# Moving a transposition from DRAM back to TensorE, and the send of wo's blocks two slots forward, in a fused attention and feed-forward kernel

## The chip, the cores and the metric

One core of one Trainium2 chip. The metric is device time in microseconds (us); lower is better. The kernel before takes 1171.03 us, the median of three runs (1169.38 to 1172.58).

## The reference, cut to what matters

x has 2048 rows of 576 numbers. Each row is normalised; the normalised rows feed both a windowed attention (32 heads of 18; each row attends to itself and to seven earlier rows at a distance of two) and a feed-forward layer of 4608 units. All is float32.

```python
xn = _layernorm(x, axis=-1)
return x + _A_ref(xn, A_wqkv, A_wo) + _B_ref(xn, B_w1, B_w2)
# _A_ref: qkv = xn @ wqkv; softmax over 8 keys (dilation 2); o @ wo
# _B_ref: relu(xn @ w1) @ w2
```

## The kernel before, in words

**Numbers.** Every float32 matrix is split into a high and a low part (`fp32r`): ScalarE writes the high part as a copy, VectorE subtracts it from the original for the low part. A product is high x high + high x low + low x high. So each value that TensorE reads needs ScalarE first and then VectorE.

**Stages.** The rows are dealt into two parities (`ph`, 0 and 1: even and odd rows of x), since the attention's distance of two never mixes them. One parity is 1024 rows: eight tiles `i` of 128 rows, or four blocks `tb` of 256. Work goes through *slots* `n` of the list `slots`: 2 parities x 12 chunks of the 4608 units x 4 blocks x 3 groups of 128 units, 288 slots. The second parity starts at slot 144. In each slot TensorE does half of a pair's *first-layer product* (`h_two`, 14 or 13 pairs of matmuls, h for two slots at once, into `ph` or `pm` banks) and one *second product* (`o_two`, into the four `po` banks). At every third slot VectorE adds the four `po` banks to x (`o_out`, the line `x<-po`); the next slot's second product needs these banks again. From slot 7 of a parity, every 24 slots, eight slots also hold a pass for queries, keys and values (`qkv_tile`), for a quarter of the heads.

**Half arrays.** From slot 7 on, matmuls come in pairs (`mm_rows`): one in the upper 64 rows of TensorE's array, one in the lower 64, into two banks at once.

**The order.** All of it is written out by hand and kept as it stands (`manual_schedule`); each engine runs its own instructions in that order, and SP issues nearly all transfers, in order too. `at(n, f)` puts f into slot n ahead of the second product, `late(n, f)` behind it. Weights are loaded into five staging buffers about four loads ahead and split at their step (`run_splits`). Attention is background work on VectorE: `run_bg(margin)` takes the next operations from the list `bg` as long as VectorE's counted time stays below TensorE's counted time plus a margin.

**wo.** At slots 122, 125, 128, 131 of a parity (144 more in the second) the attention's output is multiplied by wo inside the second product, two tiles i at each. For that the output is transposed on the way: `wo_a` (VectorE turns blocks of 32x32, `tr<-qo`), `blocks_out` (four transfers to DRAM, `turned<-tr`, L358), `wo_f` (one transfer back, the *fetch*, `xn<-turned`, L549), `wo_s` (ScalarE's high part, `k<-xn`, L558; VectorE's low parts, L559 and L560). `WO_STEPS` tells how many slots ahead of the product each of the four stands, for even and odd i.

**x of the second parity.** Around slot 144 the eight tiles of the second parity are loaded, normalised, transposed and split (`xT`). Tiles 0 to 3 go as wo's blocks do: `norm_turned` (ScalarE, two passes), `xt_a` (VectorE turns blocks), `blocks_out` (`words<-pr`), `xt_f` (three transfers back), `xt_s` (split). Tiles 4 to 7 go through TensorE: `norm` (VectorE), `make_xt` (four transposes of 128x128 and one of 128x64 on the whole array, L303 and L304, into `pm`, then the split, L308 to L318). The eight tiles of the first parity are all made with `make_xt`, in the first seven slots.

**Banks.** The pool `ps_m` holds two banks (`pm`), each a tile of its own that is taken anew for every use.

Of the kernel before, what the change touches and what calls it, by code (L numbers as in the profile page):

```python
# [44 lines left out]

# [14 lines left out]
def tile_body(ctx: ExitStack, tc: tile.TileContext, x, wqkv, wo, w1, w2, out):  # L60
# [34 lines left out]
    turned = pool("turned", 4, space=bass.MemoryType.DRAM)  # L95
    ps_o = pool("ps_o", 4, space=PSUM)
    ps_h = pool("ps_h", 2, space=PSUM)
    ps_m = pool("ps_m", 2, space=PSUM)

    f32 = lambda ap: ap.bitcast(F32)  # L100

    ident = consts.tile([P, P], F32, name="ident")
    make_identity(nc, ident)
# [27 lines left out]
        return ins  # L131

    def dve(n):
        t["dve"] += (n + 130) / 960.0


    tasks = deque()
# [143 lines left out]

    def norm(ph, i, act=False):
        nm, r = MR.pop((ph, i))
        xn = tmp.tile([P, 640], F32, name="xn", bufs=3)[:, 0:D]
        if act:
            nc.scalar.activation(xn, X[ph, i], AF.Identity, bias=nm)
            nc.scalar.activation(xn, xn, AF.Copy, scale=r)
        else:
            nc.vector.tensor_scalar(xn, X[ph, i], nm, r, op0=ALU.subtract, op1=ALU.mult)
            dve(600)  # L290
        XN[ph, i] = xn

    def transpose_split(src, hi, mix, lo, bank=None, parts=False):

        if bank is ps_o:
            pa = ps_o.tile([P, 512], F32, name="po").rearrange("p (k c) -> p k c", k=KT)
            pb = ps_o.tile([P, 512], F32, name="po")[0:DR, 0:P]
        else:
            pa = ps_m.tile([P, KT, P], F32, name="pm")
            pb = ps_h.tile([P, TBN], F32, name="ph") if bank is ps_h else ps_m.tile([P, P], F32, name="pm")  # L300
            pb = pb[0:DR, 0:P]
        for k in range(KT):
            nc.tensor.transpose(pa[:, k, :], src[:, k * P : (k + 1) * P], ident)  # L303
        nc.tensor.transpose(pb, src[:, KT * P : D], ident)  # L304
        t["pe"] += 5 * 0.06

        def high():
            nc.scalar.activation(hi, pa, AF.Copy)  # L308

        def low():  # L310
            nc.vector.tensor_tensor(lo, pa, f32(hi), op=ALU.subtract)
            dve(512)

        def last_high():
            nc.scalar.activation(mix[0:DR], pb, AF.Copy)

        def last_low():
            nc.vector.tensor_tensor(mix[DR:P], pb, f32(mix[0:DR]), op=ALU.subtract)  # L318
            dve(128)

        steps = high, low, last_high, last_low
        if not parts:
            for f in steps:
                f()
        return steps

    def make_xt(ph, i, bank=None, parts=False):
        tb, h = divmod(i, 2)
        if h == 0:
            XT[ph, tb] = xtp.tile([P, 10, TBN], F32R, name="xT")  # L330
        d = XT[ph, tb][:, :, h * P : (h + 1) * P]
        xn = XN.pop((ph, i))
        steps = transpose_split(xn, d[:, 5:9, :], d[:, 4, :], d[:, 0:4, :], bank, parts)
        if ph:
            nc.scalar.activation(d[DR:P, 9, :], f32(d[0:DR, 4, :]), AF.Copy)
        return steps

    def twin(tb):
        nc.scalar.activation(XT[0, tb][DR:P, 9, :], f32(XT[0, tb][0:DR, 4, :]), AF.Copy)
# [13 lines left out]
    def blocks_out(ph, i):  # L353

        td, tr = TD[ph, i]
        for r in range(4):
# [6 lines left out]
    def norm_turned(ph, i):  # L363
        nm, r = MR.pop((ph, i))
        z = prp.tile([P, W, UD], F32, name="pr").rearrange("p w c -> p (w c)")
        XN[ph, i] = xn, _ = z[:, 0:D], z[:, D : 2 * D]
        nc.scalar.activation(xn, X[ph, i], AF.Identity, bias=nm)
        nc.scalar.activation(xn, xn, AF.Copy, scale=r)

    def xt_a(ph, i):  # L370

        xn, tr = XN.pop((ph, i))
        nc.vector.transpose(tr, xn)
        dve(D)
        TD[ph, i] = turned.tile([D // 32, 32, P], F32, name="words"), tr

    def xt_f(ph, i):
        tb, h = divmod(i, 2)
        if h == 0:
            XT[ph, tb] = xtp.tile([P, 10, TBN], F32R, name="xT")  # L380
        z, td = f32(XT[ph, tb][:, 0:5, h * P : (h + 1) * P]), TD.pop((ph, i))[0]
        nc.sync.dma_start(z[:, 0:KT], td[0 : 4 * KT].rearrange("(k c) j i -> (c j) k i", k=KT))
        for rows in slice(0, DR), slice(DR, P):
            nc.sync.dma_start(z[rows, KT], td[4 * KT : D // 32].rearrange("c j i -> (c j) i"))

    def xt_s(ph, i):

        tb, h = divmod(i, 2)
        d = XT[ph, tb][:, :, h * P : (h + 1) * P]
        mix, z = d[:, 4, :], d[:, 9, :]  # L390
        nc.scalar.activation(d[:, 5:9, :], f32(d[:, 0:4, :]), AF.Copy)  # L391
        nc.vector.tensor_tensor(d[:, 0:4, :], f32(d[:, 0:4, :]), f32(d[:, 5:9, :]), op=ALU.subtract)
        nc.scalar.activation(z[DR:P], f32(mix[DR:P]), AF.Copy)
        nc.vector.tensor_tensor(mix[DR:P], f32(mix[DR:P]), f32(z[DR:P]), op=ALU.subtract)
        nc.scalar.activation(mix[0:DR], f32(mix[0:DR]), AF.Copy)
        dve(512)
        dve(128)

    TD = {}

# [5 lines left out]
    def qkv_tile(ph, u, i):  # L406
# [18 lines left out]

        if not second:
            for h in range(2):
                PQ[h] = ps_m.tile([P, 3, UD], F32, name="pm")
# [20 lines left out]
    def attention(ph, u):  # L449
# [129 lines left out]
    def h_terms(n, terms, other=False):  # L579
        ph, c, tb, f = slots[n]  # L580
        w, xt = W1[ph, c, f], XT[ph, tb]
        if n not in HP:
            HP[n] = ps_m.tile([P, TBN], F32, name="pm") if other else ps_h.tile([P, TBN], F32, name="ph")
# [31 lines left out]
    def h_two(g, second):  # L615


        def run(n, terms):
            ph, c, tb, f = slots[n]
            w, xt = W1[ph, c, f], XT[ph, tb]  # L620
            return [
                (HP[n], w[:, b // 5, (b % 5) * P : (b % 5 + 1) * P], xt[:, a, :], not second and j == 0, second and j == len(terms) - 1, TBN)
                for j, (a, b) in enumerate(terms)
            ]

        if not second:
            HB["m"] = not HB["m"] and not busy_m.intersection((g - 3, g - 2, g - 1))
            for n in (g, g + 1):
                HP[n] = ps_m.tile([P, TBN], F32, name="pm") if HB["m"] else ps_h.tile([P, TBN], F32, name="ph")
# [43 lines left out]
    def o_mm(n, out=True, which=range(2)):  # L673
# [18 lines left out]
        if out:  # L692
            o_out(n, which)

    def o_out(n, which=range(2), rows=False):
        ph, c, tb, f = slots[n]
        if f < C - 1:
# [8 lines left out]
        for k, h in order:  # L706
# [22 lines left out]
    for ph in range(NPH):  # L729
# [22 lines left out]
        if ph + 1 < NPH:  # L752
            e = b + SPP - SPC
            for i in range(NI):
                if i >= len(XT_STEPS):
                    z = e + 3 + 2 * i - (i == NI - 1)
                    at(z - 6, load_x, ph + 1, i)
                    at(z - 1, stats, ph + 1, i)
                    at(z, norm, ph + 1, i)
                    at(z + 1, make_xt, ph + 1, i)  # L760
                    busy_m.add(z + 1)
                    continue
                load, first, second, turn, send, back, parts = (e + k for k in XT_STEPS[i])
                at(load, load_x, ph + 1, i)
                late(first, stats, ph + 1, i, False, True)
                late(second, norm_turned, ph + 1, i)
                late(turn, xt_a, ph + 1, i)
                at(send, blocks_out, ph + 1, i)
                at(back, xt_f, ph + 1, i)
                at(parts, xt_s, ph + 1, i)  # L770
# [88 lines left out]
    def margin(n):  # L859
# [56 lines left out]
```

## Time and profile before

| what | value |
|---|---|
| median of the runs | 1171.03 us |
| the profiled execution | 1171.2 us |
| its span | 1169.5 us |
| TensorE (PE) busy | 1152.5 us, 99% |
| VectorE (DVE) busy | 804.8 us, 69% |
| ScalarE (ACT) busy | 287.7 us, 25% |
| the chain that ended last: TensorE's share | 93% |
| the same: transfers' share | 3% |
| granted TensorE clock, mean | 0.996 |

How to read it: the lines of the profile name a line of the kernel, the engine, the operation and `out<-in` by the tiles' names. PE is TensorE's matmul, PEld its loading of weights, SPq the queue in which SP issues transfers. TensorE's busy time includes matmuls that run at a lower clock, so a full row of it is not yet TensorE at its best; the pace of a slot in an undisturbed stretch is the measure. In a row of the windows view stand: the window, its length, busy time and count of PE, PEld, DVE, ACT and POOL, then the granted clock (1.00 is full), the transfers' share and GB/s. In a timeline row: start, length, engine, line, operation, count, and in brackets how long the engine had been idle and what ended it.

### The profile page before, as it was taken

To read this page: it belongs to the slowest core of one execution; us is meant where nothing else is said; L and a number is where in the kernel's file an instruction comes from. 1 tells how busy PE (TensorE), PEld (TensorE's weight loads), DVE (VectorE), ACT (ScalarE), POOL (GpSimd) and SP (SyncE) were. 2 spreads that over 40 slices of the span, in tenths; PEclk is the share of its full clock that TensorE was granted. 3 is DMA by queue.
4 is the path that set the end of the run, shared out by engine and by line. 5 is a ranking of instruction groups with operands and counts; after the bars stand their busy time and mean duration, and the time that the engine had idled before them with its cause. 6 is when DMAs were issued, how large, how long until landed. Compare 5 with 4: busy or idle time off the path is not lost.

```text
span 1169.5 us, 38344 instructions
## 1 busy us (share of the span) xinstructions
PE 1152.5 (99%) x17114; PEld 1142.7 (98%) x17114; DVE 804.8 (69%) x1457; ACT 287.7 (25%) x756; POOL 43.4 (4%) x60
## 2 busy tenths in 40 slices
PE   9999999999999999899999999999999999998998
PEld 8999999999999999899989999999999999998998
DVE  7428687878877888553663286977787878884533
ACT  5322222221222222121432122122222212221210
POOL 3200000000000000000010000000000000000000
PEclk9999999999999999999999999999999999999999
DMA  5312312311222212643552212122213222226502
GB/s 183 98 38 64 84 45 58 84 56 47 73 66 68 67 34 65 155 110 90 138 173 66 59 50 78 45 63 78 56 58 80 58 58 66 54 64 135 111 14 82
DMA packets 149940, 89.71 MB, mean 77 GB/s; under 512 B 58528, under 2 KB 133536, under 8 KB 149776
## 3 DMA queue, kind: packets, MB, share of 16 engines
q1 hardware_dynamic: 146816, 78.61, 25.5%
q10 hardware_dynamic: 2960, 8.65, 2.5%
q8 instruction: 135, 2.21, 0.8%
q14 instruction: 29, 0.24, 0.1%
HBM read 67.90 MB, written 11.14 MB: 68 GB/s over the span
## 4 chain that ended last, share of the span: by engine, by line
PE 93%; DMA 3%; SPq 1%; DVE 1%; ACT 1%; issue 1%; DVEq 0%; POOL 0%; ACTq 0%
PE po L129 40%; PE pm L129 27%; PE ph L129 22%; PE ph L119 1%; PE po L119 1%; DMA turned<-tr 1%; SPq L358 1%; DMA words<-pr 1%; DMA xn<-turned 1%; PE pm L303 1%; DVE x L709 0%; DMA xT<-words 0%; DMA x<-in_x 0%; DVE hlo L600 0%; SPq L179 0%
## 5 line engine op out<-in xcount | busy, mean ns | idle before, releaser
L129 PE MATMUL po<-w2t,hhi 64*128 64x256 f32 (+1 forms) x4448 | 450.5, 292 | 0.1
L129 PEld LDWEIGHTS po<-w2t,hhi 64*128 64x128 f32 x4448 | 365.0, 185 | 2.4 <-issue 1.2
L129 PE MATMUL po<-w2t,hlo 64*128 64x256 f32 (+1 forms) x2224 | 340.8, 290 | 0.0
L129 PE MATMUL ph<-xT,w1t 64*128 64x256 f32 x4698 | 303.4, 275 | 3.1 <-ACT xT L391 2.9
L129 PEld LDWEIGHTS ph<-xT,w1t 64*128 64x128 f32 x4698 | 291.0, 185 | 5.9 <-ACT xT L391 3.1
L709 DVE TENSOR_TENSOR x<-po,x 128x320 f32<-128x320 f32 (+1 forms) x384 | 149.7, 450 | 175.6 <-PE po L129 172.9
L129 PEld LDWEIGHTS po<-w2t,hlo 64*128 64x128 f32 x2224 | 224.3, 185 | 0.0
L129 PE MATMUL pm<-wq,xT 64*128 64x432 f32 x1728 | 180.6, 354 | 0.0
L129 PE MATMUL pm<-xT,w1t 64*128 64x256 f32 x2808 | 177.9, 273 | 0.0
L129 PEld LDWEIGHTS pm<-xT,w1t 64*128 64x128 f32 x2808 | 171.9, 184 | 0.0
L129 PEld LDWEIGHTS pm<-wq,xT 64*128 64x128 f32 x1728 | 162.5, 184 | 2.0
L597 ACT ACTIVATE hhi<-ph 128x256 fp32r<-128x256 f32 x183 | 60.8, 382 | 326.2 <-PE ph L129 294.2
L600 DVE SCALAR_TENSOR_TENSOR hlo<-ph,hhi 128x256 fp32r<-128x256 f32 x183 | 69.3, 417 | 75.6 <-ACT hhi L597 75.3
L597 ACT ACTIVATE hhi<-pm 128x256 fp32r<-128x256 f32 x105 | 34.7, 382 | 259.8 <-PE pm L129 259.3
L465 DVE TENSOR_TENSOR pr<-qo,k 128x1152 f32<-128x1152 f32 x64 | 84.9, 1350 | 2.0 <-DMA k<-k 2.0
L468 DVE TENSOR_REDUCE lg<-pr 128x64 f32<-128x1152 f32 x64 | 84.7, 1344 | 0.0
L497 DVE TENSOR_TENSOR pr<-lg,v 128x1152 f32<-128x1152 f32 x64 | 83.9, 1347 | 0.1
L434 ACT ACTIVATE k<-pm 128x144 f32<-128x144 f32 x64 | 19.3, 302 | 238.0 <-PE pm L129 191.1
L600 DVE SCALAR_TENSOR_TENSOR hlo<-pm,hhi 128x256 fp32r<-128x256 f32 x105 | 39.6, 418 | 44.3 <-ACT hhi L597 43.1
L504 DVE TENSOR_TENSOR pr<-pr 128x288 f32<-128x288 f32 (+1 forms) x128 | 69.7, 599 | 0.0
L166 DVE TENSOR_TENSOR w2t<-st,w2t 128x576 fp32r<-128x576 f32 x72 | 53.9, 749 | 16.2 <-ACT w2t L162 16.2
L166 DVE TENSOR_TENSOR w1t<-st,w1t 128x640 fp32r<-128x640 f32 x70 | 56.9, 812 | 2.2 <-ACT w1t L162 1.3
(87 smaller groups left out, 706.3 us busy)
## 6 DMA issues: line engine op xcount, KB each, us to landing
st<-in_w SPq DMA_DIRECT2D x72, 288.0 KB, 2.9
st<-in_w SPq DMA_DIRECT2D x72, 256.0 KB, 3.0
st<-in_wqkv SPq DMA_DIRECT2D x32, 216.0 KB, 3.1
turned<-tr SPq DMA_DIRECT2D x64, 80.0 KB, 2.9
xn<-turned SPq DMA_DIRECT2D x16, 320.0 KB, 3.3
st<-in_w SPq DMA_DIRECT2D x144, 32.0 KB, 2.7
out<-x SPq DMA_DIRECT2D x15, 288.0 KB, 2.5
x<-in_x SPq DMA_DIRECT2D x14, 288.0 KB, 4.1
```

Of the source, the lines that this page charges most:

```text
L119: nc.tensor.matmul(o, l, r, start=start, stop=stop)
L129: ins = nc.tensor.matmul(o, l[z], r[z], start=start, stop=stop)
L166: nc.vector.tensor_tensor(lo, src, f32(hi), op=ALU.subtract)
L303: nc.tensor.transpose(pa[:, k, :], src[:, k * P : (k + 1) * P], ident)
L434: nc.scalar.activation(k[:, W - 1 + j, :], pq[:, 1, :], AF.Copy)
L465: nc.vector.tensor_tensor(pr[i], q, window(k, i), op=ALU.mult)
L468: nc.vector.tensor_reduce(lg[:, i], pr.pop(i).rearrange(heads, d=Dh), axis=AX.X, op=ALU.add)
L497: nc.vector.tensor_tensor(pr[i].rearrange(heads, d=Dh), e, window(v, i).rearrange(heads, d=Dh), op=ALU.mult)
L504: nc.vector.tensor_tensor(o, z[:, 0:n], z[:, n : 2 * n], op=ALU.add)
L597: nc.scalar.activation(hi, pt, AF.Relu)
L600: nc.vector.scalar_tensor_tensor(lo, pt, 0.0, f32(hi), op0=ALU.max, op1=ALU.subtract)
L709: nc.vector.tensor_tensor(acc[:, cols], PO[k, h], acc[:, cols], op=ALU.add)
```

## The change

1. wo's blocks are turned and sent two slots sooner (`WO_STEPS`); fetch and split stay where they are.
2. All eight tiles of the second parity go through TensorE, in halves of 64 rows: `make_xt_rows` transposes the upper and the lower 64 rows of a tile side by side, five pairs of 64x128 blocks, into both `pm` banks. `norm` writes the last 64 columns twice, so that the fifth block has the full width. `XT_STEPS` holds the slots of load, statistics, normalisation and transposition. The way through DRAM (`norm_turned`, `xt_a`, `xt_f`, `xt_s`) goes.
3. The two `pm` banks become one tile, taken once (`two_banks`); `bank_m` hands out its halves in turn, and all former uses of the pool go through it.
4. Finished rows of x are stored one slot later (`store`).
5. The background's count: 70 instead of 130 cycles for each operation, 520 for the two reductions over the window, and another margin beside the passes for queries, keys and values.

By the built programs, SP issues 462 transfers instead of 490; TensorE has 80 transposes of 64 rows instead of 20 on the whole array; `pm` holds 101 tiles of h instead of 105.

```diff
 XT_STEPS = (
-    (-6, 0, 1, 2, 3, 4, 7),
-    (-5, 1, 2, 3, 4, 5, 8),
-    (-3, 2, 3, 4, 5, 6, 10),
-    (3, 4, 5, 6, 7, 8, 11),
+    (-6, 1, 2, 4), (-5, 2, 3, 5), (-3, 4, 5, 7), (4, 6, 7, 9),
+    (4, 8, 9, 11), (7, 10, 11, 13), (8, 12, 13, 15), (10, 13, 14, 16),
 )
-WO_STEPS = ((-5, -4, -3, -1), (-4, -3, -2, -1))
+WO_STEPS = ((-7, -6, -3, -1), (-6, -5, -2, -1))
...
-    ps_m = pool("ps_m", 2, space=PSUM)
+    ps_m = pool("ps_m", 1, space=PSUM)
+    two_banks = ps_m.tile([P, 2, 512], F32, name="pm")
+    bank_turn = [0]
+    def bank_m(n):
+        bank_turn[0] += 1
+        return two_banks[:, bank_turn[0] % 2, 0:n]
...
     def dve(n):
-        t["dve"] += (n + 130) / 960.0
+        t["dve"] += (n + 70) / 960.0
...
     def norm(ph, i, act=False):
...
+        if ph:
+            nc.vector.tensor_scalar(xw[:, D:640], X[ph, i][:, KT * P : D], nm, r, op0=ALU.subtract, op1=ALU.mult)
...
-            pa = ps_m.tile([P, KT, P], F32, name="pm")
-            pb = ps_h.tile([P, TBN], F32, name="ph") if bank is ps_h else ps_m.tile([P, P], F32, name="pm")
+            pa = bank_m(512).rearrange("p (k c) -> p k c", k=KT)
+            pb = ps_h.tile([P, TBN], F32, name="ph") if bank is ps_h else bank_m(P)
...
+    def make_xt_rows(ph, i):
+        tb, h = divmod(i, 2)
+        if h == 0:
+            XT[ph, tb] = xtp.tile([P, 10, TBN], F32R, name="xT")
+        d = XT[ph, tb][:, :, h * P : (h + 1) * P].rearrange("p k (t c) -> p k t c", t=2)
+        xn = XN.pop((ph, i))
+        pt = two_banks[:, :, 0 : 5 * 64].rearrange("p t (k c) -> p k t c", k=5)
+        for k in range(5):
+            for t_, z in enumerate((slice(0, 64), slice(64, P))):
+                nc.tensor.transpose(pt[:, k, t_], xn[z, k * P : (k + 1) * P], ident[z, z])
+        nc.scalar.activation(d[:, 5:9], pt[:, 0:KT], AF.Copy)
+        nc.vector.tensor_tensor(d[:, 0:4], pt[:, 0:KT], f32(d[:, 5:9]), op=ALU.subtract)
+        nc.scalar.activation(d[0:DR, 4], pt[0:DR, KT], AF.Copy)
+        nc.scalar.activation(d[DR:P, 9], pt[DR:P, KT], AF.Copy)
+        nc.vector.tensor_tensor(d[DR:P, 4], pt[DR:P, KT], f32(d[DR:P, 9]), op=ALU.subtract)
...
-            bg.append((0 if f is sm_exp else n + 130, f, ()))
+            bg.append((0 if f is sm_exp else n + 520 if f in (sm_max, sm_sum) else n + 70, f, ()))
...
-            elif c == NCH - 1 and (k, h) in (order[-1], order[-2 if rows else 1]):
-                nc.sync.dma_start(o_v[ph, i], acc)
+            elif end and h == 0:
+                store(ph, i)
+            elif c == NCH - 1 and h == 1 and not end:
+                at(n + 1, store, ph, i)
...
-            return (1.8 if odd else 2.7) + 2.4 * qkv - 0.8 * due
-        return (2.5 if odd else 3.5) + 2.4 * qkv - 0.8 * due
+            return (1.8 if odd else 2.7 + 2.4 * qkv) - 0.8 * due + 1.6 * (odd and qkv)
+        return (2.5 if odd else 3.5 + 2.4 * qkv) - 0.8 * due + 1.6 * (odd and qkv)
```

More of the change, by code (lines that the diff above doesn't have):

```diff
@@ L283, in norm @@
         nm, r = MR.pop((ph, i))
-        xn = tmp.tile([P, 640], F32, name="xn", bufs=3)[:, 0:D]
+        xw = tmp.tile([P, 640], F32, name="xn", bufs=3)
+        xn = xw[:, 0:D]
         if act:
@@ L332, in make_xt @@
         xn = XN.pop((ph, i))
[L333 to L336, printed above, removed]
+        return transpose_split(xn, d[:, 5:9, :], d[:, 4, :], d[:, 0:4, :], bank, parts)
+    def make_xt_rows(ph, i):
[8 more added lines that the diff above has]
+                nc.tensor.transpose(pt[:, k, t_], xn[z, k * P : (k + 1) * P], ident[z, z])
+        t["pe"] += 5 * 0.06
+        nc.scalar.activation(d[:, 5:9], pt[:, 0:KT], AF.Copy)
[3 more added lines that the diff above has]
+        nc.vector.tensor_tensor(d[DR:P, 4], pt[DR:P, KT], f32(d[DR:P, 9]), op=ALU.subtract)
+        dve(512)
+        dve(128)
     def twin(tb):
@@ L361, in blocks_out @@
             )
[L363 to L397, printed above, removed]
     TD = {}
@@ L427, in qkv_tile @@
             for h in range(2):
-                PQ[h] = ps_m.tile([P, 3, UD], F32, name="pm")
+                PQ[h] = bank_m(3 * UD).rearrange("p (s c) -> p s c", s=3)
             PQ[2] = mm_rows((run(0, LOWER_MORE), run(1, UPPER_MORE)))
@@ L582, in h_terms @@
         if n not in HP:
-            HP[n] = ps_m.tile([P, TBN], F32, name="pm") if other else ps_h.tile([P, TBN], F32, name="ph")
+            HP[n] = bank_m(TBN) if other else ps_h.tile([P, TBN], F32, name="ph")
             HN[n] = 0
@@ L628, in h_two @@
             for n in (g, g + 1):
-                HP[n] = ps_m.tile([P, TBN], F32, name="pm") if HB["m"] else ps_h.tile([P, TBN], F32, name="ph")
+                HP[n] = bank_m(TBN) if HB["m"] else ps_h.tile([P, TBN], F32, name="ph")
             HB["ins"] = mm_rows((run(g, LOWER_MORE), run(g + 1, UPPER_MORE)))
@@ L754, in tile_body @@
             for i in range(NI):
[L755 to L770, printed above, removed]
+                for k, f in zip(XT_STEPS[i], (load_x, stats, norm, make_xt_rows)):
+                    at(e + k, f, ph + 1, i)
+                busy_m.add(e + XT_STEPS[i][-1])
     for step, f, a in sorted(plan, key=lambda z: z[0]):
```

5 lines of the change are left out of this document (4 added, 1 removed).

## The prediction

> **What bounds the kernel now.** I read the page first (busy shares), then TensorE's waits, then the chain of work, then the timeline around the gaps. All TensorE times below are of one profiled execution: its span is 1169.5 us, its own time 1171.2 us (1.7 us lie around the span), and the median of the runs is 1171.03 us, so sums are made against 1171.2.
>
> From the page, from TensorE's waits, and from the chain:
>
> ```profile
> span 1169.5 us, 38344 instructions
> PE 1152.5 (99%) x17114; PEld 1142.7 (98%) x17114; DVE 804.8 (69%) x1457; ACT 287.7 (25%) x756; POOL 43.4 (4%) x60
> ```
> ```profile
> PE po L129 <- ACT k L558: 7.5, 2, 4.0
> PE ph L129 <- ACT xT L391: 2.9, 1, 2.9
> ```
> ```profile
> 447.42 1.60 PE ph L129 x28
> 459.89 1.59 PE ph L129 x28
> ```
>
> TensorE is busy 99% of the span: it is the bound, and only what it loses can be won. It waits at three places (two at wo, one between the parities). The two chain rows stand four slots apart, so an undisturbed slot is (459.89 - 447.42) / 4 = 3.12 us: this is the measure for what a disturbed stretch loses.
>
> **Part 1: turned blocks for wo sooner.** The chain's rows of the first wo slot of each parity, a later wo slot, and the timeline's starts of the two:
>
> ```profile
> 490.91 10.07 PE po L129 x123
> ...
> 525.31 8.68 PE po L129 x132
> ...
> 1071.43 9.98 PE po L129 x108
> ```
> ```profile
> 486.14 0.31 PEld L129 LDWEIGHTS po<-w2t,hhi 64*128 64x128 f32 x4
> ```
> ```profile
> 1067.16 0.31 PEld L129 LDWEIGHTS po<-w2t,hhi 64*128 64x128 f32 x4
> ```
>
> The first wo slot's second product runs from 486.14 to 490.91 + 10.07 = 500.98, 14.84 us; undisturbed it takes 8.68. Lost: 6.2 us. In the second parity: 1081.41 - 1067.16 = 14.25, lost 5.6 us; 11.8 together. That is more than the 7.5 us of waits, since the clock falls behind each gap:
>
> ```profile
> 492.00:494.00 2.00, 2.00 (x22) 2.00 (x22) 0.84 (x2) 0.00 (x0) 0.00 (x0) 0.50 0.29 79
> ```
>
> (seventh number: granted clock 0.50). What makes it late is SP's queue:
>
> ```profile
> 471.82 0.38 SPq L174 DMA_DIRECT2D st<-in_w  x1
> ...
> 472.81 0.59 SPq L179 DMA_DIRECT2D st<-in_w  x1
> ...
> 478.65 0.48 SPq L190 DMA_DIRECT2D st<-in_w  x1
> 480.34 0.38 SPq L549 DMA_DIRECT2D xn<-turned  x1
> 480.81 2.64 SPq L358 DMA_DIRECT2D turned<-tr  x4
> 483.49 1.49 SPq L174 DMA_DIRECT2D st<-in_w  x1
> ...
> 485.59 0.59 SPq L179 DMA_DIRECT2D st<-in_w  x1
> 487.00 0.38 SPq L549 DMA_DIRECT2D xn<-turned  x1
> ```
> ```profile
> 490.12 0.74 ACT L558 ACTIVATE k<-xn 128x640 fp32r<-128x640 f32 x1 [5.55 <-DMA xn<-turned]
> ```
>
> The first fetch holds the queue until the first send has landed; only then the second send goes (480.81), its blocks land just ahead of 487.00, the second fetch goes, and ScalarE gets its words at 490.12. In the changed order both first sends stand ahead of two w1 loads and a w2 load (seven issues), the very first ahead of two w2 loads more, and the first fetch only comes behind these: neither fetch waits for a landing. What is late next is SP itself. The w2 load ahead of the first fetch goes at about 478.65 (there it followed a send too), 0.5; the fetch 0.4; the third send, four DMAs, 2.3 to 2.6; the three issues of a w1 load 1.6 (471.82 to 473.40) to 2.7 (483.49 to 486.18). So the second fetch goes between 483.4 and 484.9 instead of at 487.0. With the 3.1 us from there to ScalarE's start (487.00 to 490.12) and ScalarE's 0.74, the high words are there at 487.2 to 488.7, and TensorE asks for them half a microsecond after 486.14. I take the early end, as the w1 loads around the sends are mostly of the short kind, and 0.4 us for VectorE's low words behind them: 1.0 us of wait per parity (bounds 0, and 2.8). **11.8 - 2.0 = 9.8 us won** (bounds 6 to 11.8). The two sends moved forward delay two w2 loads behind them by 2.3 us each; those are split two slots (6.2 us) after they are issued, so this costs nothing.
>
> **Part 2: x of the second parity.** Timeline and windows from slot 136's first-layer product to slot 151's:
>
> ```profile
> 562.74:620.44 57.70, 54.69 (x790) 51.77 (x788) 38.77 (x93) 23.38 (x54) 6.11 (x10) 0.97 0.59 158
> ```
>
> Fifteen slots take 57.7 us instead of 15 x 3.12 = 46.8: 10.9 us lost, by the wait of 2.9 us and the lower clock after it, four blocks of full-array transposes, and two places where VectorE's adds to x come late. The cost of a block now:
>
> ```profile
> 602.94 0.42 PEld L303 LDWEIGHTS pm<-ident,xn 128*128 128x128 f32 x4
> 602.95 0.66 PE L303 MATMUL pm<-ident,xn 128*128 128x128 f32 x4
> ...
> 603.44 0.27 PE L304 MATMUL pm<-ident,xn 128*64 128x128 f32 x1
> 603.64 0.30 PEld L129 LDWEIGHTS po<-w2t,hhi 64*128 64x128 f32 x4 [0.20 <-issue]
> ```
>
> From 602.94 to 603.64, 0.70 us, with two changes between the whole array and halves in it. New: eight blocks of five pairs of half-array transposes, no change of form. No row shows such a pair. Below: half of a 128-column transpose (0.66 less one's own 0.27, by three: 0.13), so 0.065 x 5 = 0.3 us; above: the ten one after the other at 0.13, 1.3 us. The nearest row is the pair of half-array matmuls, 1.59 / 14 = 0.11 at 256 columns; I take 0.1 a pair, 0.5 a block, **4.0 us for eight** (2.6 to 10.4). The Trainium skill (TensorEngine Tiling (Array Packing), Key Properties) says that changing the tiling mode drains TensorE; the idle 0.20 in the last row agrees.
>
> The DMA round trip through DRAM goes (28 issues), so the 2.9 us wait goes with its clock; each transposition stands six or more slots ahead of its first use. What is late next is VectorE: it now makes each block within one slot. The group rows (operations listed by form):
>
> ```profile
> L311 DVE TENSOR_TENSOR xT<-pm,xT 128x512 fp32r<-128x512 f32 x11 | 7.6, 687 | 5.5 <-ACT xT L308 5.5
> ...
> L308 ACT ACTIVATE xT<-pm 128x512 fp32r<-128x512 f32 x11 | 6.6, 598 | 13.2 <-PE pm L303 13.0
> ...
> L289 DVE TENSOR_SCALAR xn<-x,mv,rstd 128x576 f32<-128x576 f32 x10 | 5.8, 576 | 1.6 <-POOL rstd L274 1.4
> ...
> L318 DVE TENSOR_TENSOR xT<-pm,xT 64x128 fp32r<-64x128 f32 x8 | 2.3, 284 | 0.2
> L315 ACT ACTIVATE xT<-pm 64x128 fp32r<-64x128 f32 x8 | 2.1, 258 | 0.0
> ```
> ```profile
> 395.71 0.66 ACT L597 ACTIVATE hhi<-pm 128x256 fp32r<-128x256 f32 x2 [4.37 <-PE pm L129]
> ```
> ```profile
> 403.06 1.55 DVE L709 TENSOR_TENSOR x<-po,x 128x256 f32<-128x256 f32 x4
> ```
>
> Slots 137 and 143 have a block, a normalisation and the adds to x. From the end of the first-layer product: ScalarE's two relus 0.8 (0.66 and a hand-over), its 512-column copy 0.6, VectorE's subtraction 0.69, then (in the built order both of ScalarE's 64-row copies wait for that subtraction) 2 x 0.26, 0.28, normalisation 0.58 and its 64 extra columns 0.2 (an estimate from the 0.28): 3.7 us and hand-overs. Then the adds, 1.55: done at 5.4. TensorE goes on for 0.5 (block), 1.53 (second product, the rest of a slot) and 1.59 us (next first-layer product) and needs the last banks a quarter of a product later, at 4.0: a wait of about 1.4 us at slots 138 and 144 each, and by the same count 0.6 around 146 to 148: **3.4 us**. So 10.9 - 4.0 - 3.4 = **3.5 us won** (bounds: -2.9 with the dear transposes, 8.3 with the cheap ones and free adds).
>
> **Part 3: the two spare banks as one tile.** This is no move of work, but it adds waits. In the built program TensorE's transposes of x tile 2 wait no longer for their own xn but for VectorE's hlo<-pm, which reads the *other* bank: the order treats the tile as one. Its start in the timeline:
>
> ```profile
> 13.87 0.60 PE L303 MATMUL pm<-ident,xn 128*128 128x128 f32 x4
> ...
> 15.71 0.42 DVE L600 SCALAR_TENSOR_TENSOR hlo<-pm,hhi 128x256 fp32r<-128x256 f32 x1
> ...
> 25.93 0.63 PE L303 MATMUL pm<-ident,xn 128*128 128x128 f32 x4
> ...
> 26.54 0.28 DVE L318 TENSOR_TENSOR xT<-pm,xT 64x128 fp32r<-64x128 f32 x1
> ```
> ```profile
> 12.00:40.00 28.00, 27.72 (x226) 27.26 (x226) 22.73 (x59) 14.96 (x35) 10.75 (x13) 1.00 0.49 149
> ```
>
> hlo<-pm ends at 16.13, so TensorE, which is in order, stands from 14.0 to 16.2 instead of going on at 13.87: 2.3 us, and everything on it is queued behind; it has no slack there (27.7 us busy of 28). Some is caught up: 2.2 left. Tile 5's transposes (25.93) now wait for tile 4's last subtraction (26.82): 0.9, of which I keep 0.6, as the product behind it waits on VectorE in any case. Tile 7's wait for tile 6's in the same manner: 0.6 (a 64-row copy and subtraction, 0.26 + 0.28). **3.4 us lost** (0 to 5).
>
> In the steady part, of each pair of slots whose h lies in these banks (50 pairs), ScalarE's second relu now waits for VectorE's first subtraction, so the pair ends some 0.45 us later (one relu, half of 0.66, and two hand-overs). Behind it stand the adds, where there are any: they start a quarter of a product (0.38) ahead of its end at the earliest, take 1.55, and TensorE needs the last of them 1.59 + 0.38 us after that end: 0.8 us of slack, some 0.6 of it left as the adds start a little late. That covers it nearly; I put 0.5 us (0 to 4).
>
> **Part 4: budget and stores.** The background's work is the same 804.8 us, in another order. Per operation the budget is 60/960 = 0.06 us less, some six operations between two places where it is set anew: 0.4 us later at most, beside the 0.6 just named: 0 (-0.5 to 1.5). Stores issued a slot later wait less at SP's head; nobody waits for them but loads of x whose statistics are two slots off: 0.
>
> **Sum:** 1171.2 - 9.8 - 3.5 + 3.4 + 0.5 = 1161.8 us.
>
> **Rivals.**
> *Late fetch.* SP reaches the second fetch only at 485, TensorE waits 2.8 us per parity and the clock falls again (1.3 us as before): 2 x 4.1 - 2.0 = 6.2 more, 1168. For it: SP is in order, and its sends take 2.3 us each. Against: three to five loads now go between the sends and the first fetch. Chance 0.12.
> *The start's gap costs the clock.* After 2.9 us without work the clock fell to half:
>
> ```profile
> 594.00:596.00 2.00, 2.00 (x15) 1.77 (x14) 1.93 (x5) 0.00 (x0) 0.00 (x0) 0.50 1.03 361
> ```
>
> A gap of 2.2 us may do so too: 3 us at half speed, 1.6 us more, 1163.4. This lies inside the forecast. The Trainium skill (TensorE: Matmul & The Clock Gate, Part 1) puts the drop after at least one idle window of about 3.4 us; here it came after 2.9, so that bound isn't safe for 2.2.
> *The added waits cost nothing* and transposes are as cheap as the lower end: no 3.4, no 0.5, 1.4 less for the blocks: 1156.5. For it: the two operations use different banks. The Trainium skill (PSUM — Partial Sum Buffer, PSUM bank collisions raise a hardware error) asks for order only within one bank and quadrant, which would give this time; no run here shows it, and the built program waits all the same. Against: the row at 15.71 is fixed by weights that VectorE has to split first. Chance 0.15.
> *VectorE loses its slack* (the other side). If the 0.45 us of each shared pair and the 0.4 us of the looser count add up past the 0.6 us of slack, each of the 50 pairs hands 0.3 us or more to TensorE: 15 us, 1176. It decides from the point at which VectorE is over 0.2 us late ahead of such a pair. Against it:
>
> ```profile
> 397.00:459.00 62.00, 62.00 (x1014) 61.96 (x1012) 51.52 (x85) 12.18 (x30) 1.09 (x1) 1.00 0.19 52
> ```
>
> VectorE is 83% busy in this plain stretch, and 0.45 us in four slots (12.5 us) makes that 87%. Chance 0.08.
> *The change doesn't do what it says:* transposes by halves don't overlap (10.4 us instead of 4.0) and VectorE's chain grows with them: 1168.2. Chance 0.1.
>
> **How the numbers follow.** The forecast, 1161.8 with its own range 1157 to 1166, has 0.55. 0.3% (3.5 us) is about what a measurement of this kernel can tell from no change, so faster is below 1167.7 and slower above 1174.7. Faster: forecast 0.55, no cost 0.15, and about half of late fetch and of the dear transposes: 0.81. Slower: 0.08. Same: the rest, 0.11. The range goes from 1154 (the lower rival, with some of the bounds of part 2) to 1169 (late fetch and dear transposes): 1.5 in 10 left out.
>
> **What would show it.** Right: no wait of po on k over 1 us, and the first wo slot at about 9.5 us; granted clock 1.00 at both; no words queue; slots 136 to 151 in 54 us, a block at 0.5, waits on the adds to x at slots 138 and 144; a TensorE gap of about 2 us near 14 us, and the first qkv product some 3 us later than now. Wrong: a gap at wo of 2 us or more; blocks over 0.8 us; the first qkv product on time; or a plain stretch of four slots longer than 12.5 us.

## The result, and the profile after

The kernel after takes 1185.62 us (median of four runs, 1183.12 to 1186.98), beside 1171.8 of the kernel before: a ratio of 1.0118, 95% interval 1.0092 to 1.0144. It is 13.8 us **slower**; the forecast was 1161.8, with a range of 1154 to 1169 and a chance of 0.08 for slower. The profiled execution has a span of 1185.2 us (before: 1169.5). The page, with the rows that answer to those of before:

```profile
span 1185.2 us, 38329 instructions
PE 1160.7 (98%) x17174; PEld 1151.3 (97%) x17174; DVE 811.2 (68%) x1465; ACT 287.1 (24%) x748; POOL 45.1 (4%) x56
```

TensorE's waits (us in total, times, longest):

```profile
PE po L135 <- ACT k L549: 9.7, 2, 5.6
PE po L135 <- DVE x L703: 4.6, 6, 1.5
PE pm L313 <- DVE hlo L591: 2.1, 1, 2.1
PE pm L313 <- DVE xT L328: 1.9, 2, 1.0
```

The wait for wo's words, which was to go, has grown from 7.5 to 9.7 us. The wait for ScalarE's xT (2.9) has gone, and three kinds that before had at most 0.3 us each stand below. The chain of work:

```profile
967.04 5.00 DMA k<-k
972.13 2.63 DVE pr L456 x2
974.76 2.52 DVE lg L459 x2
978.96 2.53 PE po L135 x22
...
990.84 1.59 PE ph L135 x28
...
1003.30 1.59 PE ph L135 x28
...
1082.36 3.66 DMA xn<-turned
1086.84 10.38 PE po L135 x125
```

Four undisturbed slots still take 1003.30 - 990.84 = 12.46 us: the pace hasn't changed, so all of the loss lies in disturbed places. I compared slot by slot, always from the start of one first-layer product to the next: how much longer each stretch is than in the kernel before.

| stretch | before | after | forecast of the difference |
|---|---|---|---|
| from TensorE's first instruction to slot 8 | 44.7 | 49.0 | +3.4 |
| starts of attention (the stalls of the first four chain rows) and passes for queries, keys and values | | +7.5 net: single stalls of 0.5 to 1.9 us, less 0.4 to 0.5 won in six of the eight passes | +0.5 |
| the two first wo slots | 16.05 and 15.45 | 16.89 and 17.98 | -9.8 |
| 15 slots between the parities | 57.7 | 57.5 | -3.5 |

The row for these 15 slots (window, its length, busy time and count of PE, PEld, DVE, ACT, POOL, then clock), and two of the eight blocks of half-array transposes:

```profile
571.72:629.24 57.52, 54.39 (x851) 53.05 (x849) 41.18 (x99) 20.39 (x50) 6.64 (x8) 0.97 0.38 116
```
```profile
573.46 0.50 PE L355 MATMUL pm<-ident,xn 64*128 64x64 f32 x10
...
591.94 0.50 PE L355 MATMUL pm<-ident,xn 64*128 64x64 f32 x10
```

### The profile page after: what moved, and what is told of

Same layout as the page of the kernel before. It is cut to its first block, busy times and chain, and to the rows that moved or that the text cites. A ratio compares the mean times of both kernels' runs of the same rounds, so it can differ in the third digit from the quotient of the medians.

```text
span 1185.2 us, 38329 instructions
## 1 busy us (share of the span) xinstructions
PE 1160.7 (98%) x17174; PEld 1151.3 (97%) x17174; DVE 811.2 (68%) x1465; ACT 287.1 (24%) x748; POOL 45.1 (4%) x56
## 5 line engine op out<-in xcount | busy, mean ns | idle before, releaser
L135 PE MATMUL po<-w2t,hhi 64*128 64x256 f32 (+1 forms) x4448 | 462.5, 295 | 4.6 <-DVE x L703 4.6
L135 PEld LDWEIGHTS po<-w2t,hhi 64*128 64x128 f32 x4448 | 379.4, 185 | 9.8 <-DVE x L703 4.5
L135 PE MATMUL po<-w2t,hlo 64*128 64x256 f32 (+1 forms) x2224 | 354.5, 291 | 0.0
L135 PE MATMUL ph<-xT,w1t 64*128 64x256 f32 x4806 | 309.5, 275 | 0.0
L135 PEld LDWEIGHTS ph<-xT,w1t 64*128 64x128 f32 x4806 | 298.8, 185 | 0.0
L135 PEld LDWEIGHTS po<-w2t,hlo 64*128 64x128 f32 x2224 | 238.5, 186 | 0.0
L135 PE MATMUL pm<-xT,w1t 64*128 64x256 f32 x2700 | 173.3, 274 | 0.0
L135 PEld LDWEIGHTS pm<-xT,w1t 64*128 64x128 f32 x2700 | 167.1, 184 | 0.0
L588 ACT ACTIVATE hhi<-pm 128x256 fp32r<-128x256 f32 x101 | 38.9, 385 | 295.1 <-PE pm L135 258.9
L172 DVE TENSOR_TENSOR w2t<-st,w2t 128x576 fp32r<-128x576 f32 x72 | 53.9, 749 | 17.7 <-ACT w2t L168 17.6
L135 PE MATMUL po<-wq,k 64*128 64x256 f32 (+1 forms) x416 | 50.7, 303 | 9.7 <-ACT k L549 9.7
```

Of the source, the lines that this page charges most:

```text
L135: ins = nc.tensor.matmul(o, l[z], r[z], start=start, stop=stop)
L172: nc.vector.tensor_tensor(lo, src, f32(hi), op=ALU.subtract)
L588: nc.scalar.activation(hi, pt, AF.Relu)
```

## The experiments

Every ratio below is against the kernel before in runs on the same chip. Three theories answer the open questions: **Q**, that SP's own issuing bounds the fetches of wo; **T**, that the single tile costs more than forecast (its later form, T2, says where); **B**, that the looser count of the background makes the stalls.

### Undoing one part at a time

**Old steps of wo.**

```diff
-WO_STEPS = ((-7, -6, -3, -1), (-6, -5, -2, -1))
+WO_STEPS = ((-5, -4, -3, -1), (-4, -3, -2, -1))
```

> The kernel after with the steps of wo as they were before (send two slots later), all else as after. After: 1185.6 us; its first wo slots take 16.9 and 18.0 us, before's took 16.05 and 15.45. Theory Q (SP's own issuing time bounds the second fetch, so that moving the sends only moves the place where SP spends it): the wo slots go back to about 16.0 and 15.5, 3.4 us less, 1182. Rival L (the forecast: the landing of the first send bounds it, and the sooner send helps, though something else eats it): this kernel loses 3 us or more against after, 1189 or above.

Measured: 1186.54 us, ratio 1.0136 (1.0113 to 1.0158), the first wo slots 17.3 and 17.8 us. No different from after: the sooner send neither helps nor harms. The forecast's theory falls; Q is not shown by this alone, as the slots did not go back to 16.0 and 15.5.

**Two tiles again.**

```diff
+    def bank_m(n):
+        return ps_m.tile([P, 512], F32, name="pm")[:, 0:n]
...
-        pt = two_banks[:, :, 0 : 5 * 64].rearrange("p t (k c) -> p t k c", k=5)
+        pt = [bank_m(5 * 64).rearrange("p (k c) -> p k c", k=5) for _ in range(2)]
```

> The kernel after with the two pm banks as two tiles again; the split of a half-array transposition then goes bank by bank, with ten operations in place of five. Theory T (the single tile's added waits make both the slow start and the stalls of 0.5 to 1.9 us that come every 24 slots): the first qkv slot starts 4.2 us sooner, the stalls at slots 18, 42, 66, 162, 234 go (7 us), 1174. Theory B (those stalls come from the looser count of the background): only the start's 4.2 us, 1181, and the stalls stay. The ten operations may cost 1 to 2 us between slots 136 and 151 in either case.

Measured: 1175.46 us, ratio 1.0032 (1.0015 to 1.0049): 10 us back, near T. Slot 8 starts 44.7 us behind TensorE's first instruction, as before. But the larger stalls only shrink by 0.5 to 1.2 us (slot 18: 3.17 before, 4.09 after, 3.56 here), so T was right in sum and wrong in saying that they go. The wo slots gain nothing: 17.8 and 18.4 us, longer than in after.

**Old count and margins.**

```diff
-        t["dve"] += (n + 70) / 960.0
+        t["dve"] += (n + 130) / 960.0
```

(with the old margins, and the old steps of wo)

> The kernel after with the background's count and margins of before, and with the steps of wo of before (with the old count the attention's output is not ready for the sooner turn). Theory B (the looser count lets attention's first product start while keys are still in transfer, and the adds to x queue up behind it): stalls at slots 18, 42, 66, 162, 234 go, and the wo slots return to 16.0 and 15.5: 7.5 and 3.4 us less, 1175. Theory T (the single tile makes those stalls): 1182, with the stalls still there. Against the kernel that only has the old steps of wo, the difference is the count alone: 7 us by B, 0 by T.

Measured: 1184.7 us, ratio 1.0121 (1.0100 to 1.0143). Neither theory: the stalls at slots 18, 42, 66 and 162 go, as B says, and the one at 234 falls from 1.9 to 0.5 us over before; but another 0.5 us appears in six of the eight passes and at slot 105, and the wo slots stay at 17.7 and 18.7.

### SP's queue

After's timeline of SP from the first send of wo's blocks to the second fetch (start, length):

```profile
476.72 2.27 SPq L385 DMA_DIRECT2D turned<-tr  x4
479.09 0.96 SPq L196 DMA_DIRECT2D st<-in_w  x2
480.10 2.80 SPq L385 DMA_DIRECT2D turned<-tr  x4
483.00 1.47 SPq L180 DMA_DIRECT2D st<-in_w  x1
...
487.58 0.53 SPq L196 DMA_DIRECT2D st<-in_w  x1
488.21 0.38 SPq L540 DMA_DIRECT2D xn<-turned  x1
488.68 2.82 SPq L385 DMA_DIRECT2D turned<-tr  x4
491.61 1.26 SPq L180 DMA_DIRECT2D st<-in_w  x1
...
494.17 0.53 SPq L540 DMA_DIRECT2D xn<-turned  x1
```

SP issues without a break for 17.5 us. TensorE asks for the second tile's words at 498.57 - 4.04 = 494.53 (the bracket is its wait):

```profile
498.57 1.22 PE L135 MATMUL po<-wq,k 64*128 64x256 f32 x7 [4.04 <-ACT k L549]
```

The second fetch goes 0.4 us ahead of that. In the kernel before it went 0.1 us after (487.00, against 490.91 - 4.0 = 486.9); the forecast had it 2 to 3.5 ahead. Two experiments take it out of this place.

**Fetches on ScalarE's queue.**

```diff
-        nc.sync.dma_start(f32(OT[ph, i]), TD.pop((ph, i))[0].rearrange("(k c) j i -> (c j) k i", k=5))
+        nc.scalar.dma_start(f32(OT[ph, i]), TD.pop((ph, i))[0].rearrange("(k c) j i -> (c j) k i", k=5))
```

> The kernel after with the eight fetches of a parity issued by ScalarE's queue in place of SP's, at the same place of the written order. Theory Q (SP's issuing time bounds the fetches): they go when their slot comes, 4 us or more sooner, the words are there when TensorE asks, the first wo slots take about 9.5 us: 16 us less, 1170, and no wait of po on k over 1 us. Rival L (the sends' landing bounds them): ScalarE then waits itself for the landing, relus come late, wo slots stay at 16 to 18 us or grow, 1185 or above.

Measured: 1172.72 us, ratio 1.0026 (1.0011 to 1.0041): 11 us back. The wait of po on k falls from 9.7 to 2.3 us, the wo slots to 12.5 and 11.5 us:

```profile
PE po L135 <- ACT k L549: 2.3, 2, 1.6
```

That is Q's direction, but not its 9.5 us and 1170, and one wait is still over 1 us. In the first parity ScalarE did wait itself, as rival L has it: 2.75 us for the landing of a send.

**The second fetch ahead of the third send**, still on SP:

```diff
-            (at if i % 2 else late)(back, wo_f, ph, i)
+            (at if i % 2 and i > 1 else late)(back - (i == 1), wo_f, ph, i)
```

> The kernel after with the second fetch of each parity put one step forward in SP's order, right behind the first fetch and ahead of the third send (in the kernel after this send and a w1 load stand between the two fetches, 5.6 us of SP's queue). Theory Q: it goes 5 us sooner, its words come 3 us sooner or more, the first wo slots take 12 to 13 us in place of 16.9 and 18.0: 10 us less, 1175. Rival L (the landing of the words is bound by the transfers that are under way): no change, 1185.

Measured: 1173.6 us, ratio 0.9995 (0.9986 to 1.0004): 14 us back, wo slots 14.0 and 11.2. SP's row and TensorE's wait in this kernel:

```profile
489.27 1.89 SPq L540 DMA_DIRECT2D xn<-turned  x2
```
```profile
PE po L135 <- ACT k L549: 1.9, 3, 1.0
```

Nothing but the second fetch of each parity has another place in the order. Q holds in the main: the place in SP's queue counts. Against rival L, the words do land sooner, though not by as much as the fetch goes sooner: ScalarE starts on them 4.4 to 6.4 us after the second fetch's issue in these two kernels, where it was 3.6 in after (494.17 to 497.78). So part of what the queue gives back is lost to a later landing. The Trainium skill (DMA: Bandwidth & Descriptors, Issuing engines are not separate DMA queues) says that issuing from a second engine saves only the issuing engine's time. These runs are in line with it: ScalarE's queue gave 11 us, SP's reordered 14.

All the traces together say the same. Count from the first matmul of the first wo slot to the issue of the second fetch, in both parities of every kernel here:

| second fetch issued | first wo slots | length of the slot |
|---|---|---|
| 2.0 to 4.8 us before that matmul (fetch moved) | 8 | 10.3 to 14.0 us |
| 1.9 to 2.4 us after it | 7 | 15.5 to 17.2 us |
| 2.6 to 3.9 us after it | 13 | 16.7 to 18.7 us |

### One part alone

**The transposition alone** (two tiles, old count, old steps of wo, as in the diffs above):

> The kernel after with two tiles for the banks, and wo's steps and the background's count of before: of the change, the transposition by halves and the later stores remain. Theory T2 (the single tile makes the slow start, 0.5 us in each of the eight passes for queries, keys and values, and also part of the lateness at wo, since ScalarE's and VectorE's later splits hold the staging buffers that SP loads into): start and passes as before, the wo slots back at 16.0 and 15.5 us, slots 136 to 151 about as before; 1171. Rival W (something of the new transposition makes wo late): the wo slots stay at 17.7 and 18.7, 1176.

Measured: 1173.03 us, ratio 1.0002 (0.9993 to 1.0012): as T2 has it in sum. Start and passes are as before, and the 15 slots take 57.6 us. The wo slots, 17.2 and 16.7, lie between the two theories.

**One tile alone** (on the kernel before):

```diff
+    two_banks = ps_m.tile([P, 2, 512], F32, name="pm")
...
-                PQ[h] = ps_m.tile([P, 3, UD], F32, name="pm")
+                PQ[h] = bank_m(3 * UD).rearrange("p (s c) -> p s c", s=3)
```

> The kernel before with nothing changed but that its two pm banks are one tile. Theory T2: 4.2 us at the start, 0.5 in each of eight passes, 1.7 and 3.3 at the two first wo slots: 13 us more than before, 1184. Rival W: the same without the wo part, 8 us more, 1179. The forecast on record: 3.9 us more, 1175.

Measured: 1184.83 us, ratio 1.0103 (1.0088 to 1.0119): 12 us lost with nothing but this. In its profile: 5.8 us at the start, 2.9 in six of the eight passes (the first pass of each parity loses nothing), 0.8 at slots 105 and 249, 3.6 at the two wo slots, 0.7 at one start of attention, less 2.2 between the parities, where the long wait for words through DRAM is 3 us shorter; the other 1.5 us are spread over many slots. The waits at the start and in the passes are those forecast, the places are more. The row of the six passes among TensorE's waits:

```profile
PE ph L136 <- DVE hlo L607: 2.9, 6, 0.5
```

The wo part is not shown to be the tile's: in the first parity the second send held SP's queue for 4.9 us (2.6 in before), the second fetch went 1.8 us later than in before (both counted from slot 116), and that slot is 2.4 us longer. With two tiles such sends occur too (4.6 us in the kernel with two tiles again). The start (TensorE's timeline here, then after's):

```profile
16.25 0.66 PE L310 MATMUL pm<-ident,xn 128*128 128x128 f32 x4 [2.08 <-DVE hlo L607]
...
16.77 1.11 PE L126 MATMUL po<-w2t,hhi 128*128 128x256 f32 x4
```
```profile
16.21 0.65 PE L313 MATMUL pm<-ident,xn 128*128 128x128 f32 x4 [2.08 <-DVE hlo L591]
...
16.73 0.78 PE L125 MATMUL po<-w2t,hhi 128*128 128x256 f32 x4
```

The same gap of 2.1 us; behind it four matmuls take 1.11 us here and 0.78 in after. The windows view of this kernel tells why (seventh number, the granted clock):

```profile
16.00:18.00 2.00, 1.75 (x11) 1.75 (x12) 0.78 (x2) 1.05 (x3) 0.28 (x1) 0.75 1.10 343
18.00:20.00 2.00, 2.00 (x10) 2.00 (x10) 1.64 (x3) 0.27 (x1) 0.00 (x0) 0.50 0.36 103
```

So the rival "the start's gap costs the clock" came true in this profile, not in after's: 1.5 us more, where 1.6 was forecast. Windows of another length show why. In these traces the clock falls and returns only on a grid of 3.41 us, and each low stretch lasts 3.41 us or twice that (one at the end of a trace is cut off). First the kernel with one tile, then after, cut at the grid of each:

```profile
13.60:17.01 3.41, 1.33 (x13) 1.13 (x12) 3.11 (x9) 0.65 (x3) 1.02 (x1) 1.00 1.05 378
17.01:20.43 3.42, 3.42 (x17) 3.42 (x16) 1.64 (x3) 1.26 (x3) 0.00 (x0) 0.50 0.53 156
```
```profile
12.15:15.56 3.41, 1.98 (x18) 1.78 (x16) 3.28 (x9) 2.03 (x5) 0.34 (x1) 1.00 0.97 364
15.56:18.98 3.42, 2.77 (x22) 2.77 (x23) 1.89 (x5) 1.33 (x3) 0.67 (x1) 1.00 0.98 311
```

The same gap lies inside one stretch of the grid here (2.08 us idle of 3.41), and the next stretch runs at half clock; in after the grid cuts it in two (1.43 and 0.65 us idle), and the clock stays. In all traces of this case a stretch at full clock with 1.7 us idle or more was followed by one at half clock, and none with less than 1.45 us was; between these it went either way. So what the gap at the start costs depends on where the grid lies, and that differs from trace to trace.

And a pass (VectorE and ScalarE ahead of its slot, then TensorE, in the kernel with one tile; below, the kernel before):

```profile
136.47 0.39 ACT L604 ACTIVATE hhi<-pm 128x256 fp32r<-128x256 f32 x1 [4.61 <-PE pm L136]
136.89 0.42 DVE L607 SCALAR_TENSOR_TENSOR hlo<-pm,hhi 128x256 fp32r<-128x256 f32 x1 [1.86 <-ACT hhi L604]
137.34 0.39 ACT L604 ACTIVATE hhi<-pm 128x256 fp32r<-128x256 f32 x1 [0.49 <-DVE hlo L607]
137.76 0.42 DVE L607 SCALAR_TENSOR_TENSOR hlo<-pm,hhi 128x256 fp32r<-128x256 f32 x1 [0.45 <-ACT hhi L604]
...
147.44 2.21 PE L136 MATMUL ph<-xT,w1t 64*128 64x256 f32 x28 [0.48 <-DVE hlo L607]
```
```profile
131.07 0.76 DVE L600 SCALAR_TENSOR_TENSOR hlo<-pm,hhi 128x256 fp32r<-128x256 f32 x2 [1.92 <-ACT hhi L597]
```

Two low parts took 0.76 us in one go; now they take 1.29, since the second relu waits for the first low part. Those 0.5 us go through VectorE's queue (adds to x, attention, splits) to the next low part, ten microseconds later, and TensorE waits 0.48 us for it. The adds that I had named as cover are not what is late here. What slots 105 and 249 wait for is not shown here.

**The looser count alone**, and **the steps of wo with it** (both on the kernel before; the steps need the count, as attention's output isn't ready for the sooner turn without it):

```diff
-        t["dve"] += (n + 130) / 960.0
+        t["dve"] += (n + 70) / 960.0
```

> The kernel before with the change's looser count and its margins alone. Theory T2 (with two tiles the looser count is near harmless): a stall of 0.3 to 0.8 us where each attention starts, 0.4 to 0.6 us won in the passes for queries, keys and values; within 1.5 us of before. Rival B (the count makes the stalls of 0.5 to 1.9 us that the kernel after has): 5 us slower than before.

Measured: 1172.26 us, ratio 0.9990 (0.9978 to 1.0002), no loss. Stalls of 0.3 to 1.2 us at slots 18, 66, 102, 186, 210 are paid for by 0.7 us won in six of the eight passes. T2 is right.

```diff
-WO_STEPS = ((-5, -4, -3, -1), (-4, -3, -2, -1))
+WO_STEPS = ((-7, -6, -3, -1), (-6, -5, -2, -1))
```

> The kernel before with the change's steps of wo, and the count that they need. Theory Q (the first fetch stands behind all that SP issues from the first send on, the second behind a send and a w1 load, wherever the first two sends are): the second fetch goes no sooner, the first wo slots take 16 to 18 us, 0 to 3 us slower than the kernel with the count alone. The forecast on record: 9.8 us faster than it.

Measured: 1174.23 us, ratio 1.0004 (0.9994 to 1.0013), the wo slots 18.5 and 17.7 us. Counted from the start of slot 116, the second fetch goes at 22.2 us (21.0 in before), and at 21.4 in the second parity (20.6): no sooner, as Q has it. Part 1 wins nothing, on either base.

### Between the parities

**Zeroing later.** VectorE's two operations that normalise a tile (count, shortest/median/longest in ns), after:

```profile
L296 DVE TENSOR_SCALAR xn<-x,mv,rstd x14: 570/579/1166, 6.7 to 613.2; 128x576 f32<-128x576 f32 x14
L299 DVE TENSOR_SCALAR xn<-x,mv,rstd x8: 306/308/1002, 567.6 to 614.3; 128x64 f32<-128x64 f32 x8
```

The longest of both stand beside GpSimd's zeroing of k and v:

```profile
613.16 0.93 POOL L405 MEMSET k<- 1x1008 f32 x1
614.04 1.24 POOL L406 MEMSET v<- 1x1008 f32 x1
```

```diff
-            nc.gpsimd.memset(KK[ph, u][0:1, 0 : W - 1, :], 0.0)
+        late_zero = ph == 1 and u == 0
+        if i == (4 if late_zero else 0):
+            q = nc.vector if late_zero else nc.gpsimd
+            q.memset(KK[ph, u][0:1, 0 : W - 1, :], 0.0)
```

> The kernel after; in the second parity's first pass the zeroing of the two halo rows of k and v is done by VectorE four slots later, in place of GpSimd beside VectorE's normalisation of x tile 7. Theory P (VectorE and GpSimd slow each other when both run: the two operations of that normalisation took 1.17 and 1.00 us beside the zeroing, 0.58 and 0.31 elsewhere): they take 0.58 and 0.31, the adds to x come 1.3 us sooner, the slot of 6.8 us takes 3.5 to 4, and 3 us go: 1182.5. Rival: the normalisation is slow for another reason (transfers, the last tile): the two durations and the slot stay as they are, 1185.6.

Measured in a single run: 1184.89 us; the slot of 6.82 us takes 4.68, the 15 slots 54.95 in place of 57.52. The granted clock over these 15 slots is 1.00 in place of 0.97, so a part of the 2.6 us is the clock that no longer falls behind this slot. The total hardly moves because the start is 1.4 us longer here, by the clock as in the kernel with one tile; one run can't tell 1182.5 from 1185. The two rows:

```profile
L296 DVE TENSOR_SCALAR xn<-x,mv,rstd x14: 571/579/582, 6.7 to 615.4; 128x576 f32<-128x576 f32 x14
L299 DVE TENSOR_SCALAR xn<-x,mv,rstd x8: 306/308/315, 569.7 to 615.9; 128x64 f32<-128x64 f32 x8
```

P holds for the two durations: 579 and 308 ns without company, 1166 and 1002 beside GpSimd. In after's timeline these two were:

```profile
613.25 1.17 DVE L296 TENSOR_SCALAR xn<-x,mv,rstd 128x576 f32<-128x576 f32 x1 [0.44 <-POOL rstd L280]
614.33 1.00 DVE L299 TENSOR_SCALAR xn<-x,mv,rstd 128x64 f32<-128x64 f32 x1
```

The Trainium skill (SBUF — State Buffer, SBUF: two separate sides) says that VectorE, in some of its modes, which `tensor_scalar` can enter, and GpSimd share a pair of ports which one of them holds for a whole instruction while the other is blocked. The second operation ends at 615.33, just behind the second zeroing at 615.28, which agrees; the first ends 0.33 us behind the first zeroing (614.42 and 614.09), sooner than its 0.58 us would allow if it had been blocked from its start, but GpSimd's times are rough.

### Together

**Two tiles, fetches on ScalarE, the first two a slot sooner, zeroing later:**

```diff
             turn, send, back, parts = (z + k for k in WO_STEPS[i % 2])
+            back -= i < 2
```

> The kernel after with two tiles for the banks, the fetches of wo on ScalarE's queue, the first two of each parity one slot sooner, and the later zeroing. If the causes add up: start as before, no net loss in the steady part, the first wo slots at about 10 us in place of 16.0 and 15.5 (11.5 less than before), slots 136 to 151 3 to 4 us less than before, splits bank by bank 1 us more: 1157. Rival (the fetches on ScalarE hold up its relus, or the words still land late): wo slots at 12 us, 1162.

Measured: 1159.34 us, ratio 0.9887 (0.9871 to 0.9904). The wo slots take 10.3 and 11.0 us, the 15 slots 54.65. The causes add up to within 2.3 us.

**And attention a slot later:**

```diff
-            late(s + NI + 1, attention, ph, u)
+            late(s + NI + 1 + (u < NU - 1), attention, ph, u)
```

> The combined kernel (1159.3 us) with attention's background work of the first three quarters of the heads started one slot later. Theory K (the first products of attention wait for the halo rows of k still in transfer, and VectorE's low parts and adds to x queue up behind them): the stalls left at the start of attention (0.4, 1.2, 0.9 and 0.2 us) go, 2 to 3 us less, 1157. Rival: the stalls only move by a slot, or the background runs out of time before wo: 1159 or above.

Measured: 1156.81 us, ratio 0.9858 (0.9843 to 0.9872), 1.4% better than before. Three of the stalls (slots 18, 66, 162) go entirely; the one at 234 grew from 0.2 to 1.0 us. VectorE's waits of attention's first products for the transfer of k (1.2 us in two waits in the combined kernel) are gone, which agrees with K. Its page:

```profile
span 1154.9 us, 38446 instructions
PE 1146.1 (99%) x17174; PEld 1138.5 (99%) x17174; DVE 809.8 (70%) x1483; ACT 286.0 (25%) x772; POOL 41.8 (4%) x54
```

No wait of po on k is left among its waits.

## Why the prediction was wrong

| part | forecast | alone, against before |
|---|---|---|
| 1, wo sooner (with its count) | -9.8 | +0.5 (-0.7 to 1.5) |
| 2, x by half arrays, stores | -3.5 | +0.2 (-0.8 to 1.4) |
| 3, one tile | +3.9 | +12 (10 to 14) |
| 4, count | 0 | -1.2 (-2.6 to 0.2) |

Ratios times 1173 us. Part 4 is contained in the row of part 1, so the sum is 0.5 + 0.2 + 12 = 12.7; after has 13.8 (10.8 to 16.9). That the sum fits is in part luck: after loses its time in other places than one tile alone does (1.5 us less at the start, more at the starts of attention).

**Part 1 failed first at one sentence:** "The w2 load ahead of the first fetch goes at about 478.65 (there it followed a send too)". That time is from a queue in which one send and two w1 loads stood ahead of it; in the new one two sends did, and SP was never free. On before's clock (7.45 us earlier, by the start of slot 116) it went at 480.1. It failed next at "I take the early end": from this w2 load to the second fetch SP took 6.6 us (487.58 to 494.17), where the sum has 4.8 to 6.2, as the third send took 2.82 us and the w1 load behind it 2.5, the long kind. So the second fetch went at 486.7 instead of 483.4 to 484.9. The late fetch was my rival at 0.12, priced from 485; its 1.3 us for the clock is also less than my own rows leave beside the waits, (11.8 - 7.5) / 2 = 2.1. What I said of the kernel before was right, and its chain shows it: there the second fetch waits for the second send to land.

```profile
482.56 4.29 DMA turned<-tr
487.00 3.11 DMA xn<-turned
```

With the sends moved forward that wait goes, and their 5 us of issuing stand in front of the same fetch instead: the length of the queue takes the landing's place as the bound.

**Part 3 had the mechanism and not the size.** The start: 3.4 forecast, 4.2 in after's profile (the first gap close to the forecast, 2.1 for 2.2; the two later waits 1.0 us each instead of 0.6), 5.8 where the clock fell too. The 0.45 us of each pair is right (0.5), and my cover for it failed in six passes, where VectorE's queue holds attention too and hands all of it on: 2.9 us, where I had 0.5 for the whole kernel.

**Part 2 was right in most of its pieces:** slots with a block and nothing else are 0.34 to 0.38 us longer (0.5 forecast), no words queue, the slot of the long wait from 9.1 to 4.9 us, and late adds at slots 138 and 144. Missing was the normalisation beside GpSimd: without it the 15 slots take 54.95, forecast 54. So here the step that failed is "normalisation 0.58 and its 64 extra columns 0.2" for tile 7, which took 1.17 and 1.00. Where the other 0.75 us lies isn't shown.

**Part 4 was right alone, and wrong beside part 3:** with two tiles its stalls are paid back, with one tile the larger ones are 0.5 to 1.2 us longer (slot 18: 0.4 and 0.9 over before; slot 234: 0.7 and 1.9). Of the 7.5 us that after loses there, two tiles take back all, the old count 2 us, as 0.5 us in each of six passes come in place of the stalls.

**Open:** in kernels with the fetches in the written order on SP, the first wo slots lie between 15.45 and 18.7 us, in the order of the second fetch's place but without a clear order by the edit; the fourth transfer of the second send alone took 0.5 to 3.3 us to issue, and why it varies isn't known. So whether any of the 3.6 us that one tile alone loses there is the tile's isn't settled.

## What to carry over

When a transfer is late, write down everything that its issuing engine issues from now until then, in the new order, with each issue's length: moving a step forward in a full queue moves its length in front of what follows. Two banks in one tile are one thing to whoever orders the reads and writes, and each wait that this adds is to be followed through the whole in-order queue behind it, past the first slack that seems to cover it. Where two changes are needed together, test one on top of the other: the best version came from keeping the useful half of each.

## What the runs showed of the hardware

- Four transfers of wo's blocks (20 x 32 pieces of 32 numbers each) hold SP's queue for 2.3 to 3.0 us in most cases and up to 5.6 in others, and the first issue behind them can take 1.3 to 1.5 us instead of 0.4 (483.00 and 491.61 in after).
- GpSimd's zeroing of one row (0.93 and 1.24 us) lengthened VectorE's 0.58 us operation to 1.17 and its 0.31 us operation to 1.00.
- Five pairs of half-array transposes lengthen a slot by 0.34 to 0.38 us where nothing else is late.
- The granted clock changed only on a grid of 3.41 us. A gap of 2.1 us inside one stretch of the grid made the next stretch run at 0.50; the same gap cut in two by the grid (1.43 and 0.65 us) left it at 1.00.
